# First 64 queries and last 64 tokens of a causal attention moved to partitions 0 to 63, with a new order of steps

## The chip, the core and the metric

One core of one Trainium2 chip runs the whole program. The metric is the device time of one execution in microseconds (us). Before the change the median of 3 runs is 803.39 us, from 802.05 to 804.58. The engines are named as the profile names them: PE multiplies matrices (PEld is its loading of weights), DVE, ACT and POOL work on vectors, and SP issues nearly all DMAs.

## What is computed

Three layers follow one another, with 8 batches, 576 tokens and 512 features:

```python
p_packed = sm_attn(p, k, v)            # 8 heads of 64; 32 packed rows
x = sm_attn(q, p_packed, p_packed)     # all 576 queries
for e in range(4):                     # experts, two of four per token
    q, k, v = x @ wq[e], x @ wk[e], x @ wv[e]
    a = softmax(causal(q @ k.T / 8))   # 576 x 576
    out += gate(e) * (a @ v @ wo[e])
xk = mu_k * x + (1 - mu_k) * x_prev    # x is now out
xr = mu_r * x + (1 - mu_r) * x_prev
v = relu(xk @ w_k) ** 2 @ w_v
y = sigmoid(xr @ w_r) * v
```

The change lies in the causal attention of the four experts.

## The kernel before

**Stages.** From 0 to some 395 us the kernel works on the attention: for each batch `b` two groups of heads of the packed attention (`front`, L257), the experts' values (`values`, L348), queries and keys for two pairs of experts (`project`, L403), the causal attention of each expert (`soft`, L456, and `turn`, L504) and, for each pair of experts, the product with the values and the store of the result (`pair_out`, L538). Pieces of work on the last layer's weights (`fold`, L669, with `decode`, L610) lie between these steps. Then come the gates (`rstage`, L857), the first product of the last layer (`kstage`, L879) and the second (`vunit`, L921), which the change leaves alone.

**Blocks of an expert.** The 576 queries of an expert form five blocks: block 0 has 64 queries, blocks 1 to 4 have 128 each, and block i sees 64 + 128 i keys. `soft` works on a group of blocks, (0, 3), (1, 2) or (4,). PE multiplies queries by keys in two products (L475). DVE takes the scores from PSUM, adds the mask and finds the row's maximum in one instruction (L487), and writes them to a tile `ms`. ACT makes exponentials of them in place, with the row's sum (L491, one ACTIVATE and one READ_ACCUMULATOR each). `turn` then has PE transpose the exponentials 128 by 128 (L514 off the diagonal, L521 for the part on the diagonal), and ACT or DVE copies them to `tb` (L206, L208), from which `pair_out` takes them as an operand (L557).

**Halves on the diagonal.** On its diagonal, a block of 128 queries ends with 64 keys that only its last 64 queries see, on partitions 64 to 127. Block 0 lies on partitions 64 to 127 too. So that one diagonal transpose serves two blocks, ACT copies these 64 x 64 exponentials of block 0 to the free corner of block 3's `ms`, on partitions 0 to 63 (L499 to L502), and those of block 1 to the corner of block 2's: two copies for each expert of each batch, 64 in all. Six buffers `ms` of 576 go round. The diagonal transpose of group (1, 2) or (0, 3) waits for its copy.

**What sets the order.** Every step has a time in a table (`FRONT_T`, `SOFT_T`, `TURN_LAG` and so on, in units of which a batch has 20), L930 onwards. The steps are issued in the order of these times, with a priority for each kind (`PR`), and a scheduler then fixes the order of instructions on each engine. Each engine runs its list strictly in that order, and an instruction that waits holds up what stands behind it. SP's list is the list of DMAs. On PE, the second expert of a batch comes soon after the first, so its `soft` (L475) is followed after 3.4 to 4.6 us by its `turn`; for most others 6 to 15 us lie between. This holds for each of the eight batches (0 to 7). In front of this `turn` PE has the next batch's `front` (L221: first `qT` by `ppT`, then `wa` by `ppT`).

Of the kernel before, what the change touches and what calls it, by code (L numbers as in the profile page):

```python
# [23 lines left out]
FRONT_T = [-29.55, -26.81, -23.33, -16.88, -17.51, -14.04, -12.67, -12.1, -8.35]  # L24
G1_T = [1.16, 2.9, 2.88, 1.72, 1.63, 8.09, 3.77, 1.61, 3.2]
VAL_T = [-2.96, -0.14, -0.55, -0.02, 0.48]
PROJ_T = [-1.9, -1.68, 2.14, 2.7]
# [4 lines left out]
FOLD_0 = [-21.87, -18.2, -16.87, -12.45, -10.56, -6.17, -3.87, -1.87, -0.37, 1.63, 3.63, 7.17, 8.98]  # L32
FOLD_T = [5.65, 105.86]
WA_AT = -30.0
PR0, WARM = (1000, 985, 1043, 1073, 1000, 1000, 940, 980, 907), 16
WR_AT = 7.97
R_LOAD, R_RUN = ([15.94, 16.11], [22.78, 27.99])
W_AT = [4.54, 4.03]
# [18 lines left out]
def kernel(  # L57
# [5 lines left out]
    P = 128  # L63
# [77 lines left out]
    if True:  # L141
# [13 lines left out]
        qss = [ex.tile([P, TAIL + 2 * S], F32R, name=f"qs{x}", bufs=1) for x in range(2)]  # L155
        kls = [ex.tile([P, 2, S], F32R, name=f"kl{x}", bufs=1) for x in range(2)]
        mss = [ex.tile([P, S], F32, name=f"ms{x}", bufs=1) for x in range(6)]
# [14 lines left out]
        for t in vns:  # L172
            nc.vector.memset(t[:TAIL, NT - 1, :], 0.0)

# [5 lines left out]
        def zeros():  # L180
            for t in qss:
                nc.gpsimd.memset(f32(t[:, :TAIL]), 0.0)
# [4 lines left out]
            for x, t in enumerate(mss):  # L187
                nc.gpsimd.memset(t, 0.0)
                if x < len(tbs):
                    nc.gpsimd.memset(rowap(tbs[x][64:, :64], TS + P, NT - 1, 64), 0.0)  # L190
                    nc.gpsimd.memset(tbs[x][:64, (TS + P) * (NT - 1) :], 0.0)
                yield
# [64 lines left out]
        def front(b, g):  # L257


            if g == 0:  # L260
                bats[b] = {
                    n_: bt.tile([P, NG, w], F32R, tag=n_, name=nm(n_))
                    for n_, w in (("A2h", S), ("A2l", S), ("PWh", NQK), ("PWl", NQK))
                }
# [72 lines left out]
            evac("P" if b else "A", bat["A2h"][:, g, :], a2)  # L337
            small.tensor_tensor(bat["A2l"][:, g, :], a2, f32(bat["A2h"][:, g, :]), op=ALU.subtract)
            yield

        def three(bat, w, x):
            return (
                (bat["PWh"][:, :, w], bat["A2h"][:, :, x]),
                (bat["PWh"][:, :, w], bat["A2l"][:, :, x]),
                (bat["PWl"][:, :, w], bat["A2h"][:, :, x]),
            )

        def values(b):  # L348
# [3 lines left out]
            nc.gpsimd.memset(vg[:TAIL, NT - 1, :], 0.0)  # L352
            for t in range(NT):
                p0 = 0 if t < NT - 1 else TAIL
                ps = one()
                prods = three(bat, slice(QK, NQK), slice(start(t), start(t) + P))
# [9 lines left out]
                evac(E_VG, vg[p0:, t, :], ps[p0:, :VG])  # L366
# [31 lines left out]
            nc.vector.tensor_copy(ws[64:, : NT - 1, :], w[:64, : NT - 1, :])  # L398
            nc.gpsimd.tensor_copy(ws[64:, NT - 1, :], w[64:, NT - 1, :])
# [3 lines left out]
        def project(b, ep):  # L403
# [5 lines left out]
            for x in range(2):  # L409
                o = P * (2 * ep + x)  # L410
                ps = big()
                for hf in range(2):
                    i = 0
                    for ww, xx in three(bat, slice(o, o + P), slice(SH * hf, SH * hf + SH)):
# [7 lines left out]
                if x == 0:  # L422
                    z = qt[:, TAIL:].rearrange("p (e s) -> p e s", e=2)
# [17 lines left out]
            for ee in range(2):  # L441
                bat["qk", 2 * ep + ee] = (qt[:, S * ee : S * ee + TAIL + S], ks[:, ee, :], kl[:, ee, :])
# [13 lines left out]
        def soft(b, e, group):  # L456
# [12 lines left out]
            for i in group:  # L469
                n = P if i else TAIL  # L470
                kk = i * P + TAIL
# [631 lines left out]
```

## Time and profile before

| what | value |
|---|---|
| median of 3 runs (lowest, highest) | 803.39 us (802.05, 804.58) |
| the profiled execution, its own time | 801.48 us |
| its span, first to last instruction | 799.7 us |
| granted TensorE clock, mean | 0.981 of full |
| busy share of PE, DVE, ACT, POOL | 94%, 61%, 60%, 48% |
| the chain that ended last, by engine | PE 67%, DVE 16%, ACT 7%, DMA 4% |

The span and the profiled execution's time differ by 1.78 us, which lie outside the first and last instruction. A row of the timeline has a start and a length in microseconds, an engine, a line, the operation, output and input; in brackets stands the idle time of the engine just before it and what ended that. A transfer's row on SP is its issue alone; the time to its landing stands in the DMA view.

### The profile page before, as it was taken

What the parts mean: (1) busy time and instruction counts of PE and PEld (TensorE: products, weight loads), DVE (VectorE), ACT (ScalarE), POOL (GpSimd) and SP (SyncE); (2) the same over time, 40 slices, a digit from 0 to 9 for tenths busy, and PEclk for the clock granted to TensorE, in tenths of its full rate; (3) what the DMA queues carried; (4) which work ended last, traced back from release to release, by engine and by line L of the source; (5) the groups of instructions that cost most, each with busy time, mean ns of one, the idle gap of its engine ahead of it and who ended that gap; (6) DMA issues with size and microseconds to landing.
All of it is one profiled execution on the core that took longest, in us unless ns stands there. A gap on an engine that the chain in (4) does not pass through costs nothing.

```text
span 799.7 us, 15316 instructions
## 1 busy us (share of the span) xinstructions
PE 754.7 (94%) x5504; PEld 617.7 (77%) x5504; DVE 489.6 (61%) x1172; ACT 476.8 (60%) x1093; POOL 387.5 (48%) x490
## 2 busy tenths in 40 slices
PE   6788979899899999989899999999999999999998
PEld 4486957769688696869687788888888888888886
DVE  3979877987978758687867779797492111111111
ACT  2367668687786878888652523332868856656300
POOL 7357756656767644243801425451077343443700
PEclk8599999999999999999999999999999999999999
DMA  9856463464735444216456966866979655655411
GB/s 318 296 141 197 136 190 118 141 198 136 216 96 165 164 125 147 66 36 177 134 178 228 382 237 212 270 222 209 348 254 328 205 186 153 195 184 163 144 49 53
DMA packets 89836, 147.81 MB, mean 185 GB/s; under 512 B 6817, under 2 KB 61601, under 8 KB 87457
## 3 DMA queue, kind: packets, MB, share of 16 engines
q1 hardware_dynamic: 89616, 146.84, 57.2%
q8 instruction: 44, 0.72, 0.4%
q14 instruction: 32, 0.25, 0.1%
q10 hardware_dynamic: 144, 0.00, 0.0%
HBM read 87.04 MB, written 50.33 MB: 172 GB/s over the span
## 4 chain that ended last, share of the span: by engine, by line
PE 67%; DVE 16%; ACT 7%; DMA 4%; issue 3%; POOL 2%; SPq 0%; DVEq 0%; POOLq 0%; ACTq 0%
PE one L928 24%; PE one L887 8%; PE big L887 8%; PE one L867 4%; PE big L867 4%; PE one L557 4%; PE one L708 3%; ACT ms L491 3%; PE big L416 3%; DVE ms L487 3%; PE one L361 2%; PE one L514 1%; DVE kl L435 1%; PE one L475 1%; DMA vn<-in_v_dram 1%
## 5 line engine op out<-in xcount | busy, mean ns | idle before, releaser
L933 DVE TENSOR_TENSOR ring<-one,ring 128x512 f32<-128x512 f32 x36 | 24.9, 692 | 167.3 <-PE one L928 162.7
L928 PE MATMUL one<-wvh,yl 128*128 128x512 f32 x288 | 112.1, 389 | 0.0
L928 PE MATMUL one<-wvh,yh 128*128 128x512 f32 x288 | 112.1, 389 | 0.0
L928 PE MATMUL one<-wvl,yh 128*128 128x512 f32 x288 | 112.1, 389 | 0.0
L491 ACT ACTIVATE ms<-ms,nb 128x192 f32<-128x192 f32 (+4 forms) x160 | 89.3, 559 | 26.4 <-DVE nb L487 24.1
L212 POOL TENSOR_TENSOR yl<-yvh,yh 128x1024 fp32r<-128x1024 f32 (+1 forms) x24 | 49.1, 2058 | 42.0 <-ACT yh L913 24.7
L206 ACT COPY tb<-one 64x128 f32<-64x128 f32 (+5 forms) x208 | 62.1, 362 | 6.2 <-PE one L521 4.4
L639 POOL TENSOR_TENSOR dcx<-dcx,dcu 128x256 f32<-128x256 f32 x40 | 31.0, 775 | 68.9 <-DVE dcu L633 43.2
L928 PEld LDWEIGHTS one<-wvh,yl 128*128 128x128 f32 x288 | 54.1, 188 | 11.3
L928 PEld LDWEIGHTS one<-wvh,yh 128*128 128x128 f32 x288 | 54.1, 188 | 11.2
L928 PEld LDWEIGHTS one<-wvl,yh 128*128 128x128 f32 x288 | 54.1, 188 | 11.1
L487 DVE CUSTOM_DVE_ANT_0 ms<-one,mstrip 128x192 f32<-128x192 f32 (+3 forms) x128 | 51.6, 422 | 10.1 <-PE one L475 7.6
L212 POOL TENSOR_TENSOR yl<-yvl,yh 128x1024 fp32r<-128x1024 f32 x16 | 38.2, 2401 | 38.4 <-ACT yh L913 19.3
L557 PE MATMUL one<-tb,vg 128*64 128x320 f32 (+4 forms) x448 | 54.1, 366 | 2.4 <-DVE nb L487 1.4
L514 PE MATMUL one<-ident,ms 128*128 128x128 f32 x320 | 49.3, 276 | 7.3 <-ACT ms L491 6.3
L557 PEld LDWEIGHTS one<-tb,vg 128*64 128x64 f32 x448 | 32.6, 138 | 22.9 <-issue 4.0
L514 PEld LDWEIGHTS one<-ident,ms 128*128 128x128 f32 x320 | 37.0, 141 | 14.6 <-ACT ms L491 10.4
L212 POOL TENSOR_TENSOR dt<-cb 128x192 f32<-128x192 f32 (+1 forms) x48 | 31.0, 678 | 31.6 <-DVE cb L574 24.3
L1050 ACT ACTIVATE ring<-ring 128x1024 f32<-128x1024 f32 x18 | 19.1, 1060 | 35.1 <-DMA ring<-rscr 35.1
L475 PE MATMUL one<-ks,qs 128*128 128x192 f32 (+3 forms) x128 | 38.6, 328 | 0.0
L475 PE MATMUL one<-kl,qs 128*128 128x192 f32 (+3 forms) x128 | 38.2, 309 | 0.0
L660 POOL TENSOR_TENSOR wl<-wc,wh 128x256 fp32r<-128x256 f32 x48 | 35.5, 758 | 0.4
(206 smaller groups left out, 2069.7 us busy)
## 6 DMA issues: line engine op xcount, KB each, us to landing
yscr<-y SPq DMA_DIRECT2D x48, 384.0 KB, 3.5
dl<-dscr SPq DMA_DIRECT2D x40, 256.0 KB, 5.5
yvh<-yscr SPq DMA_DIRECT2D x10, 1024.0 KB, 5.4
kT<-in_k_dram SPq DMA_DIRECT2D x16, 576.0 KB, 4.4
qT<-in_q_dram SPq DMA_DIRECT2D x16, 576.0 KB, 6.7
rscr<-rr SPq DMA_DIRECT2D x12, 768.0 KB, 4.6
ring<-rscr SPq DMA_DIRECT2D x36, 256.0 KB, 2.9
out_dram<-ring SPq DMA_DIRECT2D x36, 256.0 KB, 3.2
```

Of the source, the lines that this page charges most:

```text
L206: return nc.scalar.copy(o, x)
L212: nc.gpsimd.tensor_tensor(o, x, y, op=op)
L475: nc.tensor.matmul(ps[:, po : po + kn], qs[:, i * P : i * P + P], keys[:, ko : ko + kn], start=x == 0, stop=x == 1,)
L487: nc.vector.tensor_tensor_reduce(halves(mv) if last else mv, sv, halves(mk) if last else mk, op0=ALU.add, op1=ALU.min, scale=-SC, scalar=3 ...
L491: nc.scalar.activation(mv, mv, AF.Exp, bias=nb[p0:], scale=-1.0, accum_out=bat["sums"][p0:, i, e : e + 1],)
L514: nc.tensor.transpose(ps[:, at + j * P : at + (j + 1) * P], ms[:, j * P : (j + 1) * P], ident)
L557: nc.tensor.matmul(av[64 * ee : 64 * ee + 64, qo - lo : hi - lo], vg[:, j, HD * (2 * ep + ee) : HD * (2 * ep + ee + 1)], tslice(tabs[ee], ...
L639: nc.gpsimd.tensor_add(f32(t["x"]), f32(t["x"]), f32(t["u"]))
L660: nc.gpsimd.tensor_sub(l, x, f32(h))
L867: nc.tensor.matmul(po, dx[:, NS * t + s, t0 : t0 + P], wpart("r", s, wx, t), start=n == 0, stop=n == 3 * KT - 1,)
L887: nc.tensor.matmul(po.rearrange("p (b n) -> p b n", b=2), wpart("k0" if f < 4 else "k1", s, wx, t)[:, f % 4 * P : f % 4 * P + P], dx[:, :, ...
L928: nc.tensor.matmul(ps, a[:, f, P * t : P * t + P], wres["v"][b][:, f, :], start=n == 0, stop=n == 3 * NFT - 1,)
```

## The change

Block 0 now has its 64 queries on partitions 0 to 63. Its masked scores go to a small tile `mq`, and its exponential writes straight into the corner of block 3's `ms`, so it is computed after block 3, and the copy for (0, 3) is gone. For (1, 2) the copy becomes a transfer of 64 rows of 256 bytes (16 KB), issued by SP (L501 of the changed kernel): 32 DMAs more. There are five buffers `ms` of 640 and not six of 576; `A2h` and `A2l`, made anew for each batch before, are kept, with a tail of zeros that two DVE memsets write once. The last 64 tokens lie on partitions 0 to 63 too, so block 4's diagonal is read from there. A few memsets of POOL at the start are gone. Nearly all step times are set anew, and the priority of `pair_out` goes from 100 to 236. Instructions on PE stay as many; ACT has 64 fewer, DVE two more, POOL six fewer, SP 32 more.

```diff
-FRONT_T = [-29.55, -26.81, -23.33, -16.88, -17.51, -14.04, -12.67, -12.1, -8.35]
...
+FRONT_T = [-29.98, -26.81, -23.33, -16.88, -17.51, -14.04, -12.67, -12.1, -8.35]
...
-SOFT_T = [1.76, 1.61, 2.48]
-TURN_LAG = [4.11, 4.69, 5.4]
-OUT_LAG = [3.59, 4.38, 7.43]
+SOFT_T = [1.76, 1.75, 2.48]
+TURN_LAG = [4.78, 4.58, 5.02]
+OUT_LAG = [3.59, 5.08, 7.48]
...
-E_HALF = "A"
...
-PR = {'front': 0, 'values': -100, 'project': 0, 'soft': 0, 'turn': 0, 'out': 100, 'fold': 0, 'k': 46, 'gates': 0}
+PR = {'front': 0, 'values': -100, 'project': 0, 'soft': 0, 'turn': 0, 'out': 236, 'fold': 0, 'k': 46, 'gates': 0}
...
-        mss = [ex.tile([P, S], F32, name=f"ms{x}", bufs=1) for x in range(6)]
+        mss = [ex.tile([P, S + TAIL], F32, name=f"ms{x}", bufs=1) for x in range(5)]
+        a2s = {n_: bt.tile([P, NG * S + TAIL], F32R, name=n_, bufs=1) for n_ in ("A2h", "A2l")}
...
+        for t in a2s.values():
+            nc.vector.memset(f32(t[:, NG * S :]), 0.0)
...
-            for i in group:
+            for i in sorted(group, key=lambda i: i == 0):
                 n = P if i else TAIL
+                qo = i * P - TAIL if i else 0
                 kk = i * P + TAIL
...
-                            ps[:, po : po + kn], qs[:, i * P : i * P + P], keys[:, ko : ko + kn],
+                            ps[:, po : po + kn], qs[:, qo : qo + P], keys[:, ko : ko + kn],
...
+                if i:
+                    ms = mss[turns[0] % len(mss)]
+                    turns[0] += 1
+                    mv = to = ms[:, :kk]
+                else:
+                    mv = ex.tile([P, TAIL], F32, tag="mq", name=nm("mq"))[:n]
+                    to = bat["ms", e][:n, 3 * P : 3 * P + TAIL]
...
                 nc.scalar.activation(
-                    mv, mv, AF.Exp, bias=nb[p0:], scale=-1.0,
-                    accum_out=bat["sums"][p0:, i, e : e + 1],
+                    to, mv, AF.Exp, bias=nb[:n], scale=-1.0,
+                    accum_out=bat["sums"][:n, i, e : e + 1],
                 )
...
-                evac(
-                    E_HALF, bat["ms", e, j][:64, jk - 64 : jk], bat["ms", e, i][64:, ik - 64 : ik]
-                )
+                if i == 1:
+                    first_ = ms
+                elif i == 2:
+                    nc.sync.dma_start(ms[:64, 2 * P : 2 * P + 64], first_[64:, P : P + 64])
+                if i:
+                    bat["ms", e, i] = bat["ms", e] = ms
...
-            nc.tensor.transpose(pd[:, at : at + P], ms[:, start(i) : start(i) + P], ident)
+            nc.tensor.transpose(pd[:, at : at + P], ms[:, i * P : i * P + P], ident)
...
-            k0 = 0 if i < NT - 1 else 64
...
-                pd[k0 : k0 + 64, at + P - 64 * ng : at + P].rearrange("p (x q) -> p x q", q=64),
+                pd[:64, at + P - 64 * ng : at + P].rearrange("p (x q) -> p x q", q=64),
```

**How the order moves.** Three places, each before and then after. The numbers in names are counters of tiles; line numbers differ by a few between the two kernels.

First, PE at the second expert of batch 2. `ms_116` holds block 3, `ms_119` and `ms_120` (before) or `ms_117` and `ms_118` (after) hold blocks 1 and 2, `wa,ppT` is a product of the next `front`.

```order
L221 MATMUL big_2570<-wa,ppT_2414 32x386 x8
L514 MATMUL one_2563<-ident,ms_116 128x128 x3
L514 MATMUL one_2596<-ident,ms_119 128x128
L514 MATMUL one_2596<-ident,ms_120 128x128 x2
L475 MATMUL one_2604<-ks_2314,qs_113 128x192
L475 MATMUL one_2604<-kl_115,qs_113 128x192
L475 MATMUL one_2604<-ks_2314,qs_113 128x320
L475 MATMUL one_2604<-kl_115,qs_113 128x320
L475 MATMUL big_2639<-ks_2314,qs_113 128x288
L475 MATMUL big_2639<-kl_115,qs_113 128x288
L521 MATMUL one_2596<-ident,ms_120 128x128
```

```order
L522 MATMUL one_2500<-ident,ms_116 128x128
L515 MATMUL one_2583<-ident,ms_117 128x128
L515 MATMUL one_2583<-ident,ms_118 128x128 x2
L220 MATMUL big_2550<-wa,ppT_2388 32x386 x8
L515 MATMUL one_2591<-ident,ms_119 128x128 x3
L472 MATMUL one_2602<-ks_2312,qs_113 128x192
L472 MATMUL one_2602<-kl_115,qs_113 128x192
L472 MATMUL one_2602<-ks_2312,qs_113 128x320
L472 MATMUL one_2602<-kl_115,qs_113 128x320
L522 MATMUL one_2583<-ident,ms_118 128x128
L472 MATMUL big_2626<-ks_2312,qs_113 128x288
```

The three transposes of blocks 1 and 2 off the diagonal (L514, now L515) have moved from behind block 3's to the place ahead of `wa`. Their diagonal transpose (`ms_118`) now stands ahead of the products of block 4 (`big<-ks,qs`), not in their middle.

Second, SP at the same place: `ms<-ms` is the new transfer.

```order
L243 DMA vn_126<-in_v_dram 128x4x256
L246 DMA vn_126<-in_v_dram 64x256
L248 DMA qT_2561<-in_q_dram 128x1152
L591 DMA dscr<-dt_2408 128x4x192
L248 DMA qT_2621<-in_q_dram 128x1152
L233 DMA pT_127<-in_p_dram 128x128
```

```order
L242 DMA vn_127<-in_v_dram 128x4x256
L245 DMA vn_127<-in_v_dram 64x256
L247 DMA qT_2548<-in_q_dram 128x1152
L592 DMA dscr<-dt_2401 128x4x192
L501 DMA ms_118<-ms_117 64x64
L247 DMA qT_2566<-in_q_dram 128x1152
```

The new transfer stands behind two loads of `vn`, one of `qT` and the store `dscr`, and ahead of another load of `qT`.

Third, PE in batch 1, where `pp` (L305, now L301) is a product of the packed attention and `tb,vg` belongs to `pair_out`.

```order
L514 MATMUL one_1536<-ident,ms_117 128x128 x4
L521 MATMUL one_1541<-ident,ms_117 128x128
L305 MATMUL one_1545<-ident,pp_1514 128x128
L557 MATMUL one_1555<-tb_124,vg_513 64x320
L475 MATMUL big_1485<-ks_1320,qs_112 128x288
L475 MATMUL big_1485<-kl_114,qs_112 128x288
```

```order
L515 MATMUL one_1507<-ident,ms_116 128x128 x4
L522 MATMUL one_1512<-ident,ms_116 128x128
L472 MATMUL big_1476<-ks_1319,qs_112 128x288
L472 MATMUL big_1476<-kl_114,qs_112 128x288
L472 MATMUL big_1476<-ks_1319,qs_112 128x288
L472 MATMUL big_1476<-kl_114,qs_112 128x288
L412 MATMUL big_1516<-A2h,PWh_377 128x288 x2
L412 MATMUL big_1516<-A2l,PWh_377 128x288 x2
L412 MATMUL big_1516<-A2h,PWl_378 128x288 x2
```

The last three rows come a second time, and only then the transpose of `pp`: four products of block 4 and twelve of `project` have moved ahead of it. On DVE the subtraction `l<-big,qs` (L429), which stood behind `pp`, has moved ahead of block 3's masking.

## Rows read from the trace of the kernel before

**Rows 1.** Busy time by stretch: PE, PEld, DVE, ACT, POOL; PEclk, DMA share

```profile
45.00:395.00 350.00, 323.55 (x3393) 265.77 (x3392) 275.42 (x833) 270.27 (x798) 209.33 (x326) 0.99 0.49 145
...
469.00:600.00 131.00, 131.00 (x580) 108.49 (x579) 100.86 (x152) 58.92 (x101) 55.55 (x55) 1.00 0.77 257
```

**Rows 2.** Waits of PE: line, releaser, us in total, times, longest

```profile
PE one L514 <- ACT ms L491: 6.3, 6, 2.1
```

**Rows 3.** Groups of ACT by shape: busy us, mean ns | idle before

```profile
L206 ACT COPY ms<-ms 64x64 f32<-64x64 f32 x64 | 15.4, 243 | 1.5
```

**Rows 4.** Timeline, second expert of batch 2: start us, us, engine, line

```profile
167.47 0.55 ACT L491 ACTIVATE ms<-ms,nb 128x320 f32<-128x320 f32 x1
...
168.14 0.34 ACT L491 ACTIVATE ms<-ms,nb 64x64 f32<-64x64 f32 x1
...
168.39 0.18 ACT L491 ACTIVATION_READ_ACCUMULATOR ms<-ms,nb 64x1 f32 x1
...
168.58 0.88 PE L221 MATMUL big<-wa,ppT 64*32 64x386 f32 x16 [0.51 <-DVE nb L487]
...
169.21 0.67 ACT L491 ACTIVATE ms<-ms,nb 128x448 f32<-128x448 f32 x1
...
170.02 0.87 PE L514 MATMUL one<-ident,ms 128*128 128x128 f32 x6 [0.56 <-ACT ms L491]
...
171.52 0.27 PE L521 MATMUL one<-ident,ms 128*128 128x128 f32 x1
```

**Rows 5.** Timeline in batch 1

```profile
104.10 0.75 DVE L429 TENSOR_TENSOR l<-big,qs 128x576 fp32r<-128x576 f32 x1
...
104.23 0.42 PE L305 MATMUL one<-ident,pp 128*128 128x128 f32 x1 [2.93 <-DVE pp L300]
```

**Rows 6.** Timeline of PE near the end of the attention

```profile
385.02 0.87 PE L514 MATMUL one<-ident,ms 128*128 128x128 f32 x6 [2.12 <-ACT ms L491]
...
394.52 0.74 PE L867 MATMUL big<-wrh,dh 128*128 128x512 f32 x2 [0.97 <-POOL dh L783]
```

**Rows 7.** Timeline of DVE in batch 2

```profile
153.20 0.83 DVE L633 SCALAR_TENSOR_TENSOR dcu<-raw,dce 128x256 f32<-128x256 uint32 x1
```

**Rows 8.** SP near rows 4, and landings: KB each, median us from issue

```profile
166.32 0.39 SPq L591 DMA_DIRECT2D dscr<-dt  x1
...
dscr<-dt SPq DMA_DIRECT2D x1, 384.0 KB, 6.9
...
vn<-in_v_dram SPq DMA_DIRECT2D x1, 64.0 KB, 5.0
...
pT<-in_p_dram SPq DMA_DIRECT2D x1, 64.0 KB, 1.9
```

**Rows 9.** The same place of batch 3: issue, landing, and its diagonal transpose

```profile
212.79 0.56 SPq L248 DMA_DIRECT2D qT<-in_q_dram  x1
...
qT<-in_q_dram SPq DMA_DIRECT2D x2, 576.0 KB, 7.0
...
218.01 0.27 PE L521 MATMUL one<-ident,ms 128*128 128x128 f32 x1
```

**Rows 10.** The same place of batch 4

```profile
260.17 0.37 SPq L591 DMA_DIRECT2D dscr<-dt  x1
...
dscr<-dt SPq DMA_DIRECT2D x1, 384.0 KB, 5.3
...
264.63 0.27 PE L521 MATMUL one<-ident,ms 128*128 128x128 f32 x1
```

**Rows 11.** Timeline of PE after batch 3's place

```profile
222.40 0.97 PE L557 MATMUL one<-tb,vg 128*64 128x320 f32 x6 [0.69 <-ACT tb L206]
```

**Rows 12.** Half the clock: one row of PE, and two stretches

```profile
67.22 1.58 PE L221 MATMUL big<-wa,ppT 64*32 64x386 f32 x16
...
66.80:70.20 3.40, 3.40 (x39) 1.94 (x24) 3.19 (x11) 3.16 (x10) 2.80 (x5) 0.50 0.78 236
...
104.30:107.70 3.40, 3.40 (x11) 1.75 (x13) 2.18 (x5) 1.57 (x5) 2.41 (x5) 0.50 0.54 159
```

More of the change, by code (lines that the diff above doesn't have):

```diff
@@ L180, in zeros @@
         def zeros():
-            for t in qss:
-                nc.gpsimd.memset(f32(t[:, :TAIL]), 0.0)
             for t in kls:
@@ L260, in front @@
             if g == 0:
[L261 to L264, printed above, removed]
+                bats[b] = {n_: bt.tile([P, NG, NQK], F32R, tag=n_, name=nm(n_)) for n_ in ("PWh", "PWl")}
             bat = bats[b]
@@ L336, in front, with three @@
             mark(b, g, "V", 2, nc.vector.transpose(a2, st))
-            evac("P" if b else "A", bat["A2h"][:, g, :], a2)
-            small.tensor_tensor(bat["A2l"][:, g, :], a2, f32(bat["A2h"][:, g, :]), op=ALU.subtract)
+            Ah, Al = (a2s[n_][:, S * g : S * g + S] for n_ in ("A2h", "A2l"))
+            evac("P" if b else "A", Ah, a2)
+            small.tensor_tensor(Al, a2, f32(Ah), op=ALU.subtract)
             yield
-        def three(bat, w, x):
+        def three(bat, w, o, n):
+            ah, al = (rowap(a2s[n_][:, o : o + 1], S, NG, n) for n_ in ("A2h", "A2l"))
             return (
-                (bat["PWh"][:, :, w], bat["A2h"][:, :, x]),
-                (bat["PWh"][:, :, w], bat["A2l"][:, :, x]),
-                (bat["PWl"][:, :, w], bat["A2h"][:, :, x]),
+                (bat["PWh"][:, :, w], ah), (bat["PWh"][:, :, w], al), (bat["PWl"][:, :, w], ah)
             )
@@ L413, in project @@
                     i = 0
-                    for ww, xx in three(bat, slice(o, o + P), slice(SH * hf, SH * hf + SH)):
+                    for ww, xx in three(bat, slice(o, o + P), SH * hf, SH):
                         for g in range(NG):
@@ L475, in soft @@
                         nc.tensor.matmul(
-                            ps[:, po : po + kn], qs[:, i * P : i * P + P], keys[:, ko : ko + kn],
+                            ps[:, po : po + kn], qs[:, qo : qo + P], keys[:, ko : ko + kn],
                             start=x == 0, stop=x == 1,
                         )
-                done.append((i, P - n, kk, halves(ps)[:, :, :SH] if last else ps[P - n :, at : at + kk]))
+                done.append((i, n, kk, halves(ps)[:, :, :SH] if last else ps[:n, at : at + kk]))
@@ L480, in soft @@
                 at += kk
-            for i, p0, kk, sv in done:
-                mk = mstrip[p0:, 512 + P - kk :]
-                ms = mss[turns[0] % len(mss)]
-                turns[0] += 1
+            for i, n, kk, sv in done:
+                mk = mstrip[:n, 512 + n - kk : 512 + n]
+                if i:
[5 more added lines that the diff above has]
+                    to = bat["ms", e][:n, 3 * P : 3 * P + TAIL]
@@ L508, in turn @@
             tb = bat["tb", e]
-            mss = [bat.pop(("ms", e, i)) for i in group]
+            mss = [bat.pop(("ms", e, i)) if i else None for i in group]
             ps = one()
@@ L948 @@
         add("front", call(load_wa), [WA_AT])
-        add("front", zeros(), [-6.0 + 0.5 * i for i in range(7)])
+        add("front", zeros(), [-6.0 + 0.5 * i for i in range(6)])
         add("fold", fold(), FOLD_0 + even(FOLD_T[0], FOLD_T[1], NFOLD - len(FOLD_0)))
```

50 lines of the change are left out of this document (23 added, 27 removed).

## The prediction

> **What bounds the kernel now.** I read the windows by stretch first. In the attention PE is busy 323.55 of 350 us, at a clock of 0.99; in the first product of the last layer it is busy 131.00 of 131 us, and the change touches nothing from there on [rows 1]. So the change can win only what PE stands idle between 45 and 395 us, some 26 us, in gaps of 0.3 to 2.9 us. ACT with 270.27 and DVE with 275.42 of 350 us have room on the mean: what counts is the moment at which PE waits for one of them. The waits of PE say that 6.3 us go to exponentials, in six waits [rows 2]. The groups of ACT give the half copies: 64 of 243 ns, 15.4 us in all [rows 3]. Most of these lie where nobody waits.
>
> The timeline then shows a place that comes back in every batch, the turn of the second expert [rows 4]. PE waits 0.51 us before `wa`, then 0.56 us before it may transpose, because block 3's exponential starts at 169.21 and ends at 169.88. Ahead of that exponential ACT did block 0's, 0.34 us and 0.18 us for its sum. This place decides.
>
> **The change part by part.** The sum is made against the profiled execution, 801.48 us (span 799.7 and 1.78 around it). The median of the runs is 803.39, so 1.91 us are added at the end.
>
> *Half copies gone from ACT.* 15.4 us less on an engine that has 80 us to spare in the stretch: nothing by itself. What hides it is PE's own work; if PE waited for each copy, up to 15.4 us would come back, but the waits of [rows 2] hold only 6.3 us for all exponentials together.
>
> *Block 0 behind block 3, and three transposes ahead of `wa`.* At the place of [rows 4] 0.34 + 0.18 = 0.52 us of ACT move behind block 3's exponential, which then ends at about 169.36. `wa` takes 0.88 us from 168.58, so PE is free at 169.46 and has no wait, where it began at 170.02: 0.56 us. The six transposes there take 0.87 us; three of them (0.43 us) now fill the wait of 0.51 ahead of `wa`. That is 0.99 us at most and nothing at least, if another piece delays the exponential; I take 0.7, nearer the top, as ACT's copy ahead of it stays. It counts where the diagonal transpose behind it does not wait: batches 1, 5 and 6, so 2.1 us. In the last batch the wait is 2.12 us [rows 6] and the same two terms give 0.52 + 0.43; a weight split moved ahead of the masking on DVE takes part of that back, I take 0.8. Batch 0 comes below.
>
> *The new transfer.* Its 16 KB are read and written by the same queue that carries the loads, and the diagonal transpose of blocks 1 and 2 waits for it. The trace has no transfer of this size on SP. The nearest rows are 64 KB: 1.9 us from issue to landing where little is under way, 5.0 us where a 512 KB load stands just ahead [rows 8]. At the place of [rows 4] it can be issued when block 2's exponential is done, 167.47 + 0.55 = 168.02. With 1.9 us it lands at 169.9 and nothing waits, since the transpose came at 171.52. If it lands behind what stands ahead in its queue, it must follow the store `dscr`: 166.32 + 6.9 = 173.2, and PE waits 173.2 - 171.5 = 1.7 us more than before. I take this upper value: the place is the one in which the 64 KB took 5.0 us. In batch 3 the load of `qT` stands ahead: 212.79 + 7.0 = 219.8 against 218.0, so 1.8 us [rows 9]. In batch 4 it is `dscr` again: 260.17 + 5.3 = 265.5 against 264.6, so 0.9 us [rows 10]. Together 4.4 us. In the other batches what stands ahead lands before the transpose comes. While PE waits, everything behind the transpose on PE waits too (block 4's products first), and later waits shrink because the other engines go on: batch 3 has one of 0.69 us behind the place [rows 11]. I take back 0.8, which leaves a loss of 3.6; the ends are 0 and 4.4.
>
> The Trainium skill, page "DMA: Bandwidth & Descriptors", gives a fixed cost of about 2 us for a transfer, most of it the receipt of the last write (section "Where the ~2 µs actually goes"). By that alone the transfer would be in time everywhere, and the sum would be that of the first rival; the 64 KB row with 1.9 us agrees with it, the one with 5.0 us does not.
>
> *SP's order.* On SP the transfer waits for block 2's exponential and holds up what stands behind it, here a load of `qT` that another batch needs. At this place that is under 0.5 us, on a load with several microseconds in hand: nothing. The 32 transfers move 0.5 MB, against loads of 0.5 MB each: nothing, beyond the waits above.
>
> *Batch 1.* PE waits 2.93 us for `pp` at 104.23, and `l` comes right behind it on DVE, at 104.10 [rows 5]. Now block 4's products and twelve of `project` stand ahead of it, and `l` is earlier. They use one of two large PSUM tiles, which `l` sets free, so PE still waits, but for `l` and not for the row of small steps behind it up to `pp`. The least gain is nothing, if `l` itself is late. The most is the whole 2.93 and the half clock that follows: from 104.30 to 107.70 the granted clock was 0.50, the lower of the two levels (1.2 GHz for 2.4), which costs half of 3.4 us, 1.7 [rows 12]. I take half the wait, 1.5, and 1.0 of the 1.7 for the clock, as a wait of half the length may still bring the fall: 2.5 between 0 and 4.6.
>
> *Batches 0 and 2.* Pieces of weight folding on DVE, like that of 0.83 us [rows 7], move ahead of the masking (batch 0) and of `l` and `pp` (batch 2). One such piece and a smaller part make PE 0.9 us late in batch 2; two pieces less the gain of the place (0.95) some 0.6 us in batch 0. A loss of 1.5, between 0 and 2.5.
>
> *The end.* The first gate products wait 0.97 us [rows 6]; the last expert's products now stand ahead of them and fill half: a gain of 0.5.
>
> *The rest.* Two memsets more on DVE, six less on POOL and the read of block 4's diagonal from the other partitions lie beside PE's work or cost the same. Five buffers for four blocks take the place of six for five; if one is late, a masking on DVE waits, and PE then waits for exponentials as it does now.
>
> Sum: 2.1 + 0.8 + 2.5 + 0.5 = 5.9 us won, 3.6 + 1.5 = 5.1 us lost, 0.8 us less. 801.48 - 0.8 + 1.91 = **802.6 us**. Terms of both signs nearly cancel, so the sign is open.
>
> **The rivals.**
>
> *First, the transfers land in time.* If the small transfer doesn't wait for its forerunners, or these are issued earlier under the new times, the loss of 3.6 goes and the 0.7 of batches 2, 3 and 4 come too: 802.6 - 3.6 - 2.1 = **796.9 us**. For it speaks the 1.9 us of the small load; against it the 5.0 us in just this stretch [rows 8]. The Trainium skill, same page, section "Queues, rings and completion order", says that completion is not first in, first out for one issuing engine. By that rule this rival would hold; the landings of [rows 8] speak against it, since the one small load of the stretch was as late as the large ones.
>
> *Second, slower: the clock falls behind the new waits.* In batch 1 PE idled 2.93 us just before the clock went to 0.50 [rows 5, 12]; the 2.12 us near the end [rows 6] had no such sequel, the mean of the whole stretch being 0.99 [rows 1]. At half the clock `wa` took 1.58 us and not 0.88 [rows 4, 12]. If idle times of 1.7 and 1.8 us in batches 2 and 3 bring a fall of 3.4 us each, that costs 1.7 twice: 802.6 + 3.4 = **806.0 us**, and 807.0 if the 1.0 for batch 1's clock does not come either. [...]
>
> *Third, the order does not help.* If block 3's exponential is held up by something else, the 2.1 and the 0.8 don't come: 802.6 + 2.9 = **805.5 us**. For it: ACT copies the previous transposes right before that exponential in all eight places.
>
> **How the numbers follow.** A measurement of this kernel tells some 0.3% from no change, so faster is below 801.0 and slower above 805.8. The forecast has 0.40 (own range 799.5 to 806: 0.10 faster, 0.22 same, 0.08 slower), the first rival 0.30 (0.28 faster, 0.02 same), the second 0.20 (0.03 same, 0.17 slower), the third 0.10 (0.02, 0.06, 0.02). Together 0.40 faster, 0.33 same, 0.27 slower. The range of 8 in 10 reaches from a little under the first rival to a little over the second with its addition: 796.0 to 808.5.
>
> **What would show it.** In the changed profile, PE's waits should list the diagonal transpose behind the new transfer, three times for 1 to 2.5 us, in batches 2, 3 and 4 alone; the new transfer's median to landing should be some 2 us, and 4 or more in these three. The waits of the transposes behind exponentials should fall from 6.3 to about 3.5 us. In batch 1 no wait behind `pp` should be left and the clock should stay whole. I am wrong if the transfers there land within 2 to 3 us (then the first rival), if more stretches at half the clock appear (the second), or if PE waits at other lines for more than 3 us that I did not name.

## The result and the profile after

| | before | after |
|---|---|---|
| median (lowest to highest), 5 runs each | 804.07 us (802.05 to 804.58) | 792.6 us (789.45 to 793.88) |
| profiled execution, span | 801.48, 799.7 us | 789.45, 787.7 us |
| PE idle in the span (span less PE busy) | 45.0 us | 36.1 us |

The ratio is 0.9852, with a 95% interval from 0.9825 to 0.988: 11.5 us faster, and below the low end of the forecast, 796.0 us. The profiled execution of after is its fastest; the spread of its five runs, 4.4 us, comes up again below.

The first view is the page's part 1 of the kernel before and of the changed one, the second the changed kernel's windows by stretch (length, PE, PEld, DVE, ACT and POOL busy, granted clock, DMA share, GB/s), the third its waits of PE.

```profile
PE 754.7 (94%) x5504; PEld 617.7 (77%) x5504; DVE 489.6 (61%) x1172; ACT 476.8 (60%) x1093; POOL 387.5 (48%) x490
...
PE 751.6 (95%) x5504; PEld 617.7 (78%) x5504; DVE 477.4 (61%) x1174; ACT 448.7 (57%) x1029; POOL 384.5 (49%) x484
```

```profile
45.00:395.00 350.00, 330.56 (x3433) 272.68 (x3432) 272.00 (x852) 248.45 (x750) 210.90 (x332) 1.00 0.50 148
60.00:80.00 20.00, 18.07 (x182) 11.87 (x180) 17.73 (x52) 13.82 (x42) 17.26 (x24) 1.00 0.57 177
100.00:120.00 20.00, 17.96 (x226) 12.85 (x227) 18.60 (x59) 15.69 (x47) 12.60 (x21) 1.00 0.70 210
395.00:469.00 74.00, 74.00 (x351) 60.43 (x350) 55.22 (x64) 29.00 (x50) 18.88 (x11) 1.00 0.78 279
```

```profile
PE one L522 <- DMA ms<-ms: 8.7, 7, 2.3
...
PE one L515 <- ACT ms L494: 3.0, 5, 1.5
PE one L301 <- DVE pp L296: 2.4, 3, 1.5
```

The span is 12.0 us shorter. PE is idle 8.9 us less, 8.5 of them between 45 and 470 us, and busy 3.1 us less for the same instructions. That is about what the two stretches at half the clock [rows 12] cost, 1.7 us each, and they are gone: the granted clock is 1.00 from 60 to 80 and from 100 to 120 us. Both hold although PE now waits 8.7 us for the new transfer, in seven waits. Read from this profile alone, the rest of the change saves some 18 us of idle time, and the transfer takes half of it back; the run `a_actcopy` below does not bear that out.

These waits of before, in its timeline, have no counterpart any more, or a small one:

```profile
155.04 0.30 PE L305 MATMUL one<-ident,pp 128*128 128x128 f32 x1 [1.42 <-ACT tb L206]
...
210.48 0.72 PE L221 MATMUL big<-qT,ppT 64*32 64x288 f32 x16 [1.60 <-DVE kl L435]
...
353.87 2.46 PE L557 MATMUL one<-tb,vg 128*64 128x320 f32 x16 [1.10 <-DVE nb L487]
...
459.71 0.73 PE L867 MATMUL one<-wrh,dh 128*128 128x512 f32 x2 [1.17 <-ACT dh L836]
```

The first is 0.49 us now, the third 0.44, the second and fourth are gone. At the second expert, from batch 1 on, the waits behind exponentials and ahead of `wa` [rows 4] are gone too, but for 0.22 us in batch 2, and 0.22 and 0.80 in the last batch. In batch 1, where PE waited 1.07 us behind a masking and then 2.93 us for `pp` [rows 5], 0.37 us behind a masking and 0.78 for `l` are left. From 395 to 469 us PE is busy throughout: the 0.97 [rows 6], 0.35 and 1.17 us of the gates are gone.

At the second expert of batch 2 the changed kernel shows this, PE's timeline first, then SP's, then the DMA view of the two issues (KB each, us from issue to landing):

```profile
162.59 0.31 PE L472 MATMUL one<-kl,qs 128*128 128x320 f32 x1
163.80 0.33 PE L522 MATMUL one<-ident,ms 128*128 128x128 f32 x1 [0.91 <-DMA ms<-ms]
```

```profile
157.35 0.93 SPq L592 DMA_DIRECT2D dscr<-dt  x1
160.62 0.47 SPq L501 DMA_DIRECT2D ms<-ms  x1
```

```profile
dscr<-dt SPq DMA_DIRECT2D x1, 384.0 KB, 6.2
ms<-ms SPq DMA_DIRECT2D x1, 16.0 KB, 3.1
```

The transfer is issued at 160.62 and lands at 163.7, just behind `dscr`, which was issued at 157.35 and lands at 163.6. PE waits 0.91 us for it.

### The profile page after: what moved, and what is told of

Its sections match the earlier page's. It is cut to its first block, busy times and chain, and to the rows that moved or that the text cites. A ratio compares the mean times of both kernels' runs of the same rounds, so it can differ in the third digit from the quotient of the medians.

```text
span 787.7 us, 15356 instructions
## 1 busy us (share of the span) xinstructions
PE 751.6 (95%) x5504; PEld 617.7 (78%) x5504; DVE 477.4 (61%) x1174; ACT 448.7 (57%) x1029; POOL 384.5 (49%) x484
## 4 chain that ended last, share of the span: by engine, by line
PE 74%; DVE 11%; DMA 5%; POOL 4%; ACT 3%; issue 2%; SPq 0%; POOLq 0%; DVEq 0%; ACTq 0%
PE one L929 25%; PE big L888 8%; PE one L888 8%; PE one L557 5%; PE big L412 4%; PE one L868 4%; PE big L868 4%; DMA ms<-ms 4%; PE one L709 3%; PE one L357 3%; PE one L515 2%; PE one L472 2%; DVE ms L490 2%; ACT ms L494 1%; PE big L220 1%
## 5 line engine op out<-in xcount | busy, mean ns | idle before, releaser
L494 ACT ACTIVATE ms<-ms,nb 128x192 f32<-128x192 f32 (+3 forms) x128 | 78.4, 616 | 21.3 <-DVE nb L490 21.2
L515 PE MATMUL one<-ident,ms 128*128 128x128 f32 x320 | 53.1, 281 | 3.1 <-ACT ms L494 3.0
L490 DVE CUSTOM_DVE_ANT_0 ms<-one,mstrip 128x192 f32<-128x192 f32 (+2 forms) x96 | 43.5, 481 | 15.9 <-PE one L472 15.2
L515 PEld LDWEIGHTS one<-ident,ms 128*128 128x128 f32 x320 | 36.2, 141 | 13.5 <-ACT ms L494 8.3
L472 PE MATMUL one<-ks,qs 128*128 128x192 f32 (+3 forms) x128 | 36.6, 300 | 0.4 <-ACT vg L205 0.3
L522 PE MATMUL one<-ident,ms 128*128 128x128 f32 x96 | 27.4, 287 | 9.3 <-DMA ms<-ms 8.7
```

Of the source, the lines that this page charges most:

```text
L472: nc.tensor.matmul(ps[:, po : po + kn], qs[:, qo : qo + P], keys[:, ko : ko + kn], start=x == 0, stop=x == 1,)
L490: nc.vector.tensor_tensor_reduce(halves(mv) if last else mv, sv, halves(mk) if last else mk, op0=ALU.add, op1=ALU.min, scale=-SC, scalar=3 ...
L494: nc.scalar.activation(to, mv, AF.Exp, bias=nb[:n], scale=-1.0, accum_out=bat["sums"][:n, i, e : e + 1],)
L515: nc.tensor.transpose(ps[:, at + j * P : at + (j + 1) * P], ms[:, j * P : (j + 1) * P], ident)
```

## The experiments

Two theories stand at the start. *Order*: the new order (block 0 behind block 3, and the step times) removed PE's waits. *Relief*: ACT's 64 copies less did. Under both, the transfer's price is open. "Structure" below means all of the change but the step times.

One thing holds for most edits below: the scheduler then fixes the order anew. In the kernels as built, between 160 and 270 of PE's 4562 instructions stand elsewhere than in the change after each of `a_actcopy`, `a_actq`, `a_copyall`, `a_mix` and `a_nudge1`. What such a run differs by belongs to the edit and this new order together.

### One part alone

**The step times alone** (`b_times`): the kernel before with the new tables.

```diff
-SOFT_T = [1.76, 1.61, 2.48]
+SOFT_T = [1.76, 1.75, 2.48]
...
```

> The kernel before with the new step times and priority alone. Theory 'times': 793 to 798 us, as the waits of 2.93, 1.60 and 1.10 us in batches 1, 3 and 6 and 2.5 us at the end go. Rival 'structure': 801 us or more.

799.94 us, ratio 0.9957 (0.9943 to 0.9971): a third of the gain.

**The structure alone** (`a_oldtimes`): the changed kernel with the old tables, the same lines the other way round.

```diff
-SOFT_T = [1.76, 1.75, 2.48]
+SOFT_T = [1.76, 1.61, 2.48]
...
```

> The changed kernel with the old step times and the old priority of the output step. Theory 'times' (the new step times carry the gain): 800 us or more. Rival 'structure' (block 0 behind block 3 and the copies gone carry it): 791 to 796 us.

806.72 us, ratio 1.0031 (1.0013 to 1.0048): slower than before. PE waits 7.8 us for the transfer (8.8 with one of 1.0 that the view puts down to `ks`, which landed 0.8 us after PE had gone on), and 6.3 us for `pp`.

**Block 0 behind block 3 alone** (`b_zerolast`), and the same **with the new step times** (`b_zl_times`), both with all 64 copies on ACT.

```diff
-            for i in group:
+            for i in sorted(group, key=lambda i: i == 0):
...
-                (i, _, ik, _), (j, _, jk, _) = done
+                (i, _, ik, _), (j, _, jk, _) = sorted(done, key=lambda d: d[0])
```

> The kernel before with block 0 masked and exponentiated behind block 3, all else as before (old step times, all 64 copies). Theory 'order of blocks': the waits of the second expert behind exponentials go, 6.3 us become 3 or less, 798 to 801 us. Rival 'times': with the old step times other waits take their place, 802 us or more.

> The kernel before with block 0 behind block 3 and the new step times, but with block 0 on partitions 64 to 127 and all 64 half copies on ACT, no transfer. Theory 'order' (block order and step times together carry the gain): 790 to 795 us, PE idle near 30 us. Theory 'relief' (the copies gone from ACT are needed): 797 us or more, with waits behind exponentials and copies.

805.69 us, ratio 1.0021 (1.0008 to 1.0035), and 803.88 us, ratio 0.9996 (0.9986 to 1.0006). In the second, PE's list at the second expert of batch 2 is the one shown for the change ahead of the prediction (where block 3 is `ms_119`, and not `ms_116`), and still nothing is won. Neither part carries the gain, nor do these two together: *order* as I had put it falls.

**Block 0 ahead again** (`a_zerofirst`): the changed kernel without `sorted` (`for i in group:` again), the corner taken from the next buffer. Block 3's masked scores then overwrite block 0's exponentials in the corner, so that part of the attention is left out, and block 3's masking has to wait for block 0's exponential.

> The changed kernel with block 0 ahead of block 3 again, all else changed. Theory 'order of blocks': 2 to 4 us lost, 795 to 797 us, as PE waits again for block 3's exponential in seven batches. Rival: nothing, 791 to 793 us, the step times alone removed those waits.

822.98 us, ratio 1.025 (1.0222 to 1.0279); PE waits 21.1 us for the transfer. It tells nothing about the two theories: with the exponential written straight into the corner, block 0 behind block 3 is forced, not a choice.

### The copies

**Block 0's copy back on ACT** (`a_copy03`, the transfer stays), and **both copies back** (`a_copyall`, no transfer).

```diff
-                    to = bat["ms", e][:n, 3 * P : 3 * P + TAIL]
+                    to = mv
...
-                )
+                ); i or evac("A", bat["ms", e][:n, 3 * P : 3 * P + TAIL], mv)
```

> The changed kernel with the exponentials of block 0 made in place and copied by ACT into block 3's corner (32 copies of 64 x 64 more on ACT, on the same partitions); the transfer for blocks 1 and 2 stays. Theory 'relief' (the copies gone from ACT are what lets the new order work): half of the gain is lost or more, 796 to 800 us. Rival 'order': 791 to 794 us.

> The changed kernel with both half copies back on ACT (64 more instructions), no transfer; partitions, buffers, kept operands and step times as changed. Theory 'relief': the whole gain goes, 801 to 805 us, as in the kernel before with block order and step times alone. Rival (partitions, buffers and kept operands carry the gain): 791 to 796 us.

798.88 us, ratio 0.9955 (0.9934 to 0.9976), and 796.16 us, ratio 0.9917 (0.9892 to 0.9941). Block 0's 32 copies are worth about 4 us in the kernel without a transfer (796.2 against 792.3, next run) and 6 us in the one with it. So *relief* has a share, but with all copies back two thirds of the gain stay: *relief* as I had put it falls as well.

### The transfer

**A copy on ACT in its place** (`a_actcopy`).

```diff
-                    nc.sync.dma_start(ms[:64, 2 * P : 2 * P + 64], first_[64:, P : P + 64])
+                    evac("A", ms[:64, 2 * P : 2 * P + 64], first_[64:, P : P + 64])
```

> The changed kernel with the transfer of blocks 1 and 2 replaced by a copy on ACT. Theory 'order' (the gain came from the new order of steps and from block 0 behind block 3, and the transfer gives 8.7 us of it back in waits of PE): the waits behind the transfer vanish, ACT does 32 copies of 0.24 us more beside PE's work, 784 to 788 us. Theory 'relief' (the gain came from taking 64 copies off ACT): half of the gain goes, 797 to 799 us.

792.27 us, ratio 0.9861 (0.9842 to 0.9879): the time of the change, which neither theory had expected. All 8.7 us of waits for the transfer are gone, yet PE is idle 34.3 us, not 27: other waits, of up to 1.8 us each, behind masking and `l`, have come. PE is also busy 3.7 us more, with the granted clock at 0.50 from 102.5 to 105.9 us. So the transfer costs as much here as the 32 copies that it replaces, with the order that comes with them.

**Another queue** (`a_actq`): the same transfer, issued from ACT.

```diff
-                    nc.sync.dma_start(ms[:64, 2 * P : 2 * P + 64], first_[64:, P : P + 64])
+                    nc.scalar.dma_start(ms[:64, 2 * P : 2 * P + 64], first_[64:, P : P + 64])
```

> The changed kernel with the transfer issued from ACT's queue, not SP's. Theory 'queue' (the transfer is late because it lands behind what SP issued ahead of it): it lands 1.6 to 2.5 us after its issue everywhere, PE's waits for it fall from 8.7 us to under 3, 786 to 790 us, less what 32 issues cost ACT. Rival 'load' (the DMA engines are busy whatever the queue): landings of 3 to 7 us stay in batches 2 to 5 and at the end, PE's waits stay at 6 us or more, 791 to 794 us.

806.42 us, ratio 1.0038 (1.0023 to 1.0052): a miss. At the second expert of batch 2, the issues on SP and ACT, the landings and PE's wait:

```profile
162.94 0.33 SPq L247 DMA_DIRECT2D qT<-in_q_dram  x1
...
163.70 0.47 ACTq L501 DMA_DIRECT2D ms<-ms  x1
...
168.18 0.33 PE L522 MATMUL one<-ident,ms 128*128 128x128 f32 x1 [2.21 <-DMA ms<-ms]
```

```profile
qT<-in_q_dram SPq DMA_DIRECT2D x1, 576.0 KB, 5.0
ms<-ms ACTq DMA_DIRECT2D x1, 16.0 KB, 4.4
```

The load of `qT`, issued on SP at 162.94, lands at 167.9, and the transfer, from the other queue, at 168.1, right behind it. Of the 32 transfers 30 land behind all that SP had issued ahead of them, and the other two 0.2 us ahead of the last of these: the other queue was no way past the backlog. And as SP no longer waits for the exponential, that load now goes ahead of the transfer, where before it went behind: PE's waits for the transfer grow from 8.7 to 13.6 us. That is not all of the loss: PE is also busy 7.5 us more than in the change's first profile, with three stretches of 3.4 us at half the clock where that has none, and waits 2.7 us in the gates. The Trainium skill, page "DMA: Bandwidth & Descriptors", section "Issuing engines are not separate DMA queues", says that DMAs run on the same 16 engines whoever issues them, and interleave. The run agrees with the first, with the 0.2 us between the two landings; that interleaving brings a small transfer in early it does not show.

**Less ahead of it** (`a_wr94`): four loads of 512 KB in the last batch are issued behind the transfer.

```diff
-WR_AT = 7.41
+WR_AT = 9.4
```

> The changed kernel with the four loads of 512 KB of the gate weights at the end of the attention issued later (7.41 to 9.4 units), behind the last batch's first transfer and not ahead of it; 15 of 4562 instructions of PE change their place. Theory 'backlog' (the transfer lands when the bytes issued ahead of it have landed): its landing there falls from 7.6 to under 3 us, the wait of 2.3 us goes, 789 to 791 us. Rival (the gates then wait for their weights): 793 us or more.

795.03 us, ratio 0.9901 (0.9873 to 0.9929): not faster. The DMA views of the change (with the last of the four loads alone) and of this run for the stretch show what happened:

```profile
wrl<-wscrr SPq DMA_DIRECT2D x1, 512.0 KB, 8.1
...
ms<-ms SPq DMA_DIRECT2D x1, 16.0 KB, 7.6
```

```profile
wrl<-wscrr SPq DMA_DIRECT2D x4, 512.0 KB, 7.5
ks<-ks SPq DMA_DIRECT2D x2, 144.0 KB, 9.1
ms<-ms SPq DMA_DIRECT2D x1, 16.0 KB, 2.8
```

```profile
PE one L522 <- DMA ms<-ms: 5.2, 5, 1.7
PE big L472 <- DMA ks<-ks: 3.8, 1, 3.8
```

The transfer lands after 2.8 us and not 7.6, and its wait of 2.3 us is gone, as the backlog theory has it. But now the keys' transfers `ks` stand behind the loads and land after 9.1 us, and PE waits 3.8 us for them, up to 378.1 us; from 378.2 to 381.6 the granted clock is 0.50. The backlog has only found another victim. **Both step times** (`a_best`, this one and that of `a_nudge3` below) gave 793.7 us, ratio 0.9889 (0.9865 to 0.9912), with the same new wait of 4.1 us.

> The changed kernel with the later loads of the gate weights and with the third part of the values earlier or later as in the run that set it back (-0.55 units). If both gains add: 787 to 790 us, below both kernels. Rival: 791 to 793 us, no better than the change.

**A copy on ACT at the bad places only** (`a_mix`): for the second expert and in the last batch.

```diff
+                    if e == 1 or b == B - 1:
+                        evac("A", ms[:64, 2 * P : 2 * P + 64], first_[64:, P : P + 64])
+                    else:
```

> The changed kernel with a copy on ACT in place of the transfer for the second expert of each batch and for all of the last batch, where PE waits for the transfer; 21 transfers stay. If the waits for the transfer are a real loss and little else moves: they fall from 8.7 to about 0.5 us and the kernel takes 784 to 787 us, under both kernels. Rival (a copy on ACT at just these places costs as much, as with the copy everywhere): 790 to 793 us.

797.25 us, ratio 0.9913 (0.9895 to 0.9931), slower than either forecast. No wait for the transfer is left; one of 4.0 us behind a masking in batch 1 and two stretches at half the clock, 10.2 us in all, have come, with some 270 of PE's 4562 instructions in other places.

### The order

**One step time back** (`a_nudge1`, and `a_nudge3` with another).

```diff
-SOFT_T = [1.76, 1.75, 2.48]
+SOFT_T = [1.76, 1.61, 2.48]
```

```diff
-VAL_T = [-3.35, 0.36, -1.9, 0.35, 0.62]
+VAL_T = [-3.35, 0.36, -0.55, 0.35, 0.62]
```

> The changed kernel with one step time set back (the scores of blocks 1 and 2, from 1.75 to 1.61 units); nothing is added or left out, some 200 of 4562 instructions of PE change their place. Theory 'fitted order' (the step times fit this very order, and small moves cost microseconds): 794 us or more. Rival (the order is worth what its parts are worth): 791.5 to 793.5 us.

> The changed kernel with another step time set back (the third part of the values, from -1.9 to -0.55 units); nothing is added or left out. Theory 'fitted order': 794 us or more. Rival: 791.5 to 793.5 us.

802.74 us, ratio 0.9991 (0.9973 to 1.001): the whole gain gone. And 791.22 us, ratio 0.9852 (0.9828 to 0.9875): nothing lost. In the first, PE's and SP's lists around the second expert of batch 2 are those of the change, and PE runs within 0.3 us of it up to the last product ahead of the transpose, and there within 0.1. Then, in its timelines and windows:

```profile
155.43 1.62 SPq L245 DMA_DIRECT2D vn<-in_v_dram  x1
160.67 0.47 SPq L501 DMA_DIRECT2D ms<-ms  x1
...
165.56 0.48 PE L522 MATMUL one<-ident,ms 128*128 128x128 f32 x1 [2.62 <-DMA ms<-ms]
169.07 1.21 PE L220 MATMUL big<-kT,pT 64*32 64x288 f32 x16
```

```profile
164.90:168.30 3.40, 2.75 (x12) 2.66 (x13) 0.76 (x3) 1.71 (x6) 0.00 (x0) 0.50 0.07 29
168.30:171.70 3.40, 3.40 (x27) 2.14 (x26) 3.40 (x10) 3.15 (x10) 1.34 (x2) 0.50 0.06 16
```

The issue of the load of `vn` takes 1.62 us (0.80 in the change's first profile), what stands behind it lands later, the transfer too, and PE waits 2.62 us, not 0.91. From 164.9 to 171.7 us the granted clock is 0.50; a product of `front` takes 1.21 us there and 0.71 in the change. But this late landing is not the edit's. In `a_same` below, which is the change itself once more, the same issue is nearly as long, and the wait is 2.01 us:

```profile
155.08 1.51 SPq L245 DMA_DIRECT2D vn<-in_v_dram  x1
```

Against that profile (793.55 us) the one of `a_nudge1` (803.88 us) has only 0.8 us more of waits for the transfer, but 6.8 us more at half the clock, which cost 3.4, and 3.7 us of waits in the gates, where the change has none:

```profile
402.03 0.74 PE L868 MATMUL one<-wrh,dh 128*128 128x512 f32 x2 [1.68 <-DVE nb L490]
...
462.11 0.73 PE L868 MATMUL one<-wrh,dh 128*128 128x512 f32 x2 [1.53 <-ACT dh L837]
```

Why one step time brings these is not shown.

**The same step time back, with a copy on ACT for the transfer** (`n1_act`, the first edit of these two and that of `a_actcopy`).

> The changed kernel with the one step time set back that cost ten microseconds (scores of blocks 1 and 2, 1.75 to 1.61 units) and with a copy on ACT in place of the transfer. Theory 'transfer' (that loss came through longer waits for the transfer and half the clock behind them): most of it comes back, 791 to 795 us. Rival 'order alone' (the moved instructions cost it): 800 us or more.

790.86 us, ratio 0.9855 (0.9828 to 0.9882). All 11.9 us come back when the transfer is taken out, and from 394 to 470 us PE is busy throughout again. So the loss of `a_nudge1` comes only together with the transfer, as far as that can be told from an order in which some 190 of PE's instructions stand elsewhere.

**The transfer's price in two more orders**: the structure with the old step times and a copy on ACT (`a_old_actcopy`, the edits of `a_oldtimes` and `a_actcopy`), and the kernel before with the transfer alone (`b_transfer`).

```diff
-                evac(
+                (evac if i == 0 else lambda _, o, x: nc.sync.dma_start(o, x))(
                     E_HALF, bat["ms", e, j][:64, jk - 64 : jk], bat["ms", e, i][64:, ik - 64 : ik]
                 )
```

> The changed kernel with the old step times and a copy on ACT in place of the transfer. Theory 'transfer' (what an order loses, it loses mainly through the transfer's waits and the clock behind them): 796 to 801 us, against 806.7 with the transfer. Rival 'times' (the old order itself costs it): 804 us or more.

> The kernel before with the copy for blocks 1 and 2 made by a transfer of SP, all else as before (old step times, block 0 ahead and copied by ACT). Theory 'transfer': waits of PE for it of 5 to 9 us in the same batches, 806 to 811 us. Rival (the copy taken off ACT gains as much): 801 to 804 us.

799.99 us, ratio 0.9952 (0.9938 to 0.9966), and 806.5 us, ratio 1.0036 (1.0018 to 1.0054). In the second the view puts 3.5 us of PE's waits down to the transfer, but one more is the transfer's, as PE's timeline and the DMA view of the issues at 264.49 (`ms`) and 265.05 us (`qT`) show:

```profile
269.66 0.33 PE L521 MATMUL one<-ident,ms 128*128 128x128 f32 x1 [2.43 <-DMA qT<-in_q_dram]
```

```profile
qT<-in_q_dram SPq DMA_DIRECT2D x1, 576.0 KB, 5.8
...
ms<-ms SPq DMA_DIRECT2D x1, 16.0 KB, 5.1
```

The load lands at 270.9, 1.2 us after PE has gone on, and the transfer at 269.6. So PE waits 5.9 us for it, as much as expected. The clock adds to that, with four stretches at half of it, 17.0 us in all, where the kernel before has two of 3.4 us; but this profile is of the slowest of the eight runs (809.87 us).

| order | with the transfer | with a copy on ACT | price |
|---|---|---|---|
| the change | 792.6 | 792.3 | 0.3 |
| the change, one step time back | 802.7 | 790.9 | 11.9 |
| structure, old step times | 806.7 | 800.0 | 6.7 |
| before | 806.5 | 803.7 | 2.8 |

The two of a row differ in the order too, by some 190 to 230 of PE's 4562 instructions, and the first price is within the noise.

**The change once more** (`a_same`, no edit).

> The changed kernel as it is, once more, for a second profile and more times. If the waits for the transfer and the clock behind them vary from one execution to the next: 789 to 794 us again, and this profile has other lengths of these waits than 0.9 to 2.3 us, or a stretch at half the clock behind one. Rival: the same lengths and no such stretch.

791.96 us, ratio 0.9854 (0.9827 to 0.9881), runs from 787.97 to 795.0. This profile, of a run of 793.55 us, has other waits for the transfer, and in batch 4 half the clock behind one:

```profile
PE one L522 <- DMA ms<-ms: 9.7, 7, 2.6
```

```profile
258.22 0.33 PE L522 MATMUL one<-ident,ms 128*128 128x128 f32 x1 [2.12 <-DMA ms<-ms]
```

```profile
260.00:263.00 3.00, 3.00 (x25) 1.46 (x10) 3.00 (x9) 3.00 (x13) 0.44 (x1) 0.50 0.10 27
```

Batch 1's wait is 1.47 us here and 0.94 in the first profile, batch 2's 2.01 and 0.91, batch 5's 0.73 and 1.82. The same program, the same order: how long the backlog takes varies, and behind one of these waits the clock falls.

## Why the prediction was wrong, point by point

*Where the kernel could win* was right: nearly all of the gain lies in PE's idle time between 45 and 470 us (8.5 of 8.9 us) and in the two stretches at half the clock.

*The transfer's waits*: right in mechanism, and in place for three waits of seven; too small in size. I took 4.4 us less 0.8, in batches 2, 3 and 4. The profile has 8.7, with 0.91, 0.91 and 1.52 us there, but also 0.94 and 1.82 in batches 1 and 5, which I had written down as free, and 2.29 in the last. In batch 1, for one, the transpose comes 1.1 us sooner after the expert's first scores, as the waits ahead of it are gone, and `dscr` lands 5.7 us after its issue, not 4.7; in the last batch four loads of 512 KB stand ahead of it. The upper end that I chose was the better one of the two: it lands behind what stands ahead of it. None of SP's 449 transfers landed before one issued ahead of it. The Trainium skill, page "DMA: Bandwidth & Descriptors", section "Where the ~2 µs actually goes", gives some 2 us of fixed cost, as a best fit to transfers that GpSimd issues; for these of SP it holds where little is under way (1.6 us at the least), not in the median of 2.7 or where the backlog is long (7.6).

*The places of the second expert*: 2.9 us of gain predicted for batches 1, 5, 6 and the last. PE's waits there for exponentials and ahead of `wa` fell from 5.2 us in batches 1 to 6 to 0.2, and from 2.1 to 1.0 in the last. Undersized: also in batches 2 to 4 these waits went, though the transfer's took their place.

*Batch 1*: 2.5 us. Measured: 1.07 and 2.93 us became 0.37 and 0.78, and the clock's 1.7 came back: 4.6 us, the upper end, less a new wait of 0.56 for `l`.

*Batches 0 and 2, the step that failed first*: a loss of 1.5 us "between 0 and 2.5". In batch 2 the wait for `pp` fell from 1.42 to 0.49 us, where I had it grow by 0.9; in batch 0 PE is idle 0.4 us more, but its stretch at half the clock is gone, which is worth 1.7. I had charged the pieces of weight folding that moved ahead with their full length, and had not asked whether something that they were waiting behind had moved as well. The bound excluded a gain without a reason.

*The end*: 0.5 us, measured 2.5 (0.97, 0.35 and 1.17 us, all gone). *Not named at all*: 1.60 us in batch 3 and 0.66 of the 1.10 in batch 6. The first goes with the step times: it is gone in `b_times`, and `a_oldtimes` has 1.81 there. The second goes with the structure: `b_times` still has the 1.10, `a_oldtimes` 0.44. The lines are of `a_oldtimes`, of `b_times` and again of `a_oldtimes`:

```profile
212.91 0.72 PE L220 MATMUL big<-qT,ppT 64*32 64x288 f32 x16 [1.81 <-issue]
...
352.13 1.22 PE L557 MATMUL one<-tb,vg 128*64 128x320 f32 x4 [1.10 <-DVE nb L487]
...
359.17 1.16 PE L557 MATMUL one<-tb,vg 128*64 128x320 f32 x8 [0.44 <-DVE nb L490]
```

These sit outside the two or three places whose order I compared.

*Half copies gone from ACT*: nothing predicted. Block 0's 32 copies, put back, cost some 4 us (`a_copyall`) or 6 (`a_copy03`), with the order that came with them; those of blocks 1 and 2, put back for the transfer, cost nothing (`a_actcopy`).

*Added up*, the places named so far give 8.4 us of the 12.0 by which the span is shorter: 5.0 and 1.1 at the second expert, 4.0 in batch 1, 2.2 in batches 0 and 2, 2.5 at the end and 2.3 not named, less 8.7 for the transfer. Smaller waits between 45 and 395 us give 3.5 more: fourteen with 5.0 us before, four with 1.5 after. So the steps of the sum that failed are these: the loss of 1.5 us in batches 0 and 2, where 2.2 were won; all that I had not read, put at nothing, where some 5.8 were won; the second expert, batch 1 and the end, each too small; and, the other way, the transfer's 3.6, where PE waited 8.7. That is the wider fault: the sum priced what moves at the places I had read, and set the rest of a table in which nearly every step time is new to nothing.

*The rivals.* The first had the nearest time (796.9) by luck, for a reason that does not hold, as the transfers are late. I had taken it to hold if completion is not first in, first out; but that no order is promised does not mean that a small transfer overtakes, and none of SP's did. The second, the clock falling behind the new waits, did not happen in the profiled execution but does happen: in `a_same` behind 2.12 us, in `a_nudge1` behind 2.62 and 1.95. It is a part of what the transfer costs in an order next to this one: 3.4 of the 10.3 us between these two profiles. The third is ruled out by the waits for exponentials, 6.3 us before and 3.0 after, where the forecast had said 3.5.

**What explains the gain.** Along one path without transfers it comes in these steps: structure with old step times and a copy on ACT 800.0 us, 3.7 below the kernel before in that comparison; with the new step times 792.3, another 7.7; the transfer in place of the last 32 copies, nothing. Taken alone on the old structure the step times gave 3.6. So structure and step times belong together: each is worth some 4 us by itself, and 11.4 together, provided that the transfer does not spoil it. Left open is why the new step times with the old partitions, buffers and all copies (`b_zl_times`, 803.9) differ by 7.7 us from the change with all copies (`a_copyall`, 796.2), though all but some 10 of PE's 4562 instructions stand in the same order: which of partitions, kept operands and buffers does it was not tried. In their profiles, 802.5 and 793.7 us long, 4.0 of the 8.8 us are PE's busy time, with three stretches at half the clock against one. And no version ran that is clearly faster than the change: `n1_act` with 790.9 us is below both kernels, but its interval is nearly that of the change.

## What to carry to other kernels

In this kernel a small transfer between on-chip buffers landed when the bytes issued ahead of it had landed, and another queue did not help: price it by the backlog at its place (here 1.6 us to 7.6), not by its size, and ask what takes its place in the queue if you move the backlog. Where PE waits for it, try a copy on a compute engine: the transfer cost 0.3 to 11.9 us more than the copy in four orders, and one step time moved changed the time by 10.1 us with the transfer, by 1.4 with the copy. Take a second profile of the same program before you put a wait down to an edit: the wait in batch 2 was 0.91 us in one and 2.01 in the other. And where a table of step times is new throughout, go through every wait of the profile before pricing the change, not only the places where its purpose lies; a term may be a gain until a row excludes it.

## What the runs showed of the hardware

I had not expected the other queue to make PE wait longer for the transfer, 13.6 us against 8.7, with the landing in batch 2 0.2 us behind SP's load. Nor had I expected one program's landings to differ so much between executions: the wait in batch 2 was 0.91 us in one and 2.01 in the other, under the same order. The clock went to 0.50 behind waits of 1.95, 2.12 and 2.62 us, and behind one of 1.94 us in batch 0 of the kernel before, but not behind 2.29 (the change), 2.34 (`a_nudge1`) and 2.57 us (`a_same`): the length of a wait alone does not tell.
